# The probabilities of 16 attention units scaled by a plain multiplication instead of one that also sums

## The chip, the cores and the metric

One core of a Trainium2 chip runs the whole program in one launch. The metric is the device time in microseconds, from the median of several runs. Five engines work side by side, each through its own queue in order: TensorE (PE, and PEld for its weight loads), VectorE (DVE), ScalarE (ACT), GpSimd (POOL) and SyncE (SP), which here only issues transfers.

## What is computed

The reference chains three blocks over 4 batches of 576 tokens. The attention block has 8 heads of 64 columns and a mask in blocks of 64 tokens; its output feeds a gated two-layer block, and that a second one with a token mix.

```python
scores = scale * np.matmul(q, k.transpose(0, 1, 3, 2))
scores = np.where(mask, scores, -1000000000.0)
scores = scores - np.max(scores, axis=-1, keepdims=True)
attn = np.exp(scores)
attn = attn / (np.sum(attn, axis=-1, keepdims=True) + 1e-09)
attn_out = np.matmul(attn, v)
# first block (x: attention output, heads side by side; xk, xr: mixes of x and x shifted by a token)
k = np.maximum(xk @ w_k, 0.0)
x = sigmoid(xr @ w_r) * (k * k @ w_v)
# second block
h = gelu(x @ w_in); u, v = split(h)
out = x + (u * (w_sg @ layernorm(v) + b_sg)) @ w_out
```

## The kernel before

**Units.** Attention is cut into 64 units: a batch, a head, and the low (tokens 0 to 319) or high half of its queries. They run in the order low halves of batches 0 and 1 (units 0 to 15), high halves of batches 0 and 1 (16 to 31), then the same for batches 2 and 3. For the first 16 units (`n < DIRECT`, with `DIRECT = 16`) queries and keys are multiplied as plain float32; later ones are split into a rounded part and a remainder, which costs POOL, ACT and DVE more work (`split_qk`, `split_v`).

**One unit.** `emit_S` gives PE the score products in three chunks of 64, 128 and 128 queries. DVE takes the row maximum (L348), ACT scales it (L350) and takes the exponential with its row sum (L355), and `norm` follows on DVE: the row sums get their 1e-9 (L360), the reciprocal is taken (L361), and each chunk of the probabilities P is multiplied in place by its row's reciprocal (L365). That last instruction is `tensor_scalar` with a second operation and `accum_out=junk`: it also writes a row sum, into `junk`, which nothing reads. Then `emit_T` transposes P on PE (L387), ACT copies the result from PSUM to SBUF (L393, recorded at the helper L167), and `emit_PV` multiplies with the values. A P buffer serves every second unit (`P_89` and `P_90` in the listings of the order).

**The first block beside it.** While the first units run, 20 tiles of weights (8 of `w_k`, 4 of `w_r`, 8 of `w_v`) are loaded by SP and split into a float32r pair by `w_split`: ACT takes the absolute value (L228), DVE does two plain one-source instructions (L229, L230) and two with two sources (L232, L234) on 128x512, ACT rounds (L237), and POOL subtracts (L178, `w<-u,w`). The first block's products are then `M<-xh,w` and `M<-xl,w` (with `w_k` and `w_r`) and `M<-kh,w` and `M<-kl,w` (with `w_v`, 96 for each half batch). `xh`/`xl` and `kh`/`kl` are further float32r pairs; POOL and DVE share their remainders (L178), and L501 on DVE mixes the tokens.

**What sets the order.** The program is written in an order that a small planner makes (class `Order`: due times of the work of the other engines against PE's estimated time), and the tile framework's scheduler, with `schedule_with_timeline_sim=True`, then orders every engine's queue by a timeline of its own estimates. When the cost of one kind of instruction changes, rows change places on every engine, far from the edit too. SP's queue is in order as well: a load whose buffer is not yet free holds all loads behind it.

The lines quoted most:

```python
nc.vector.tensor_scalar(out=P[0:m, o:o + e], in0=P[0:m, o:o + e],
                        scalar1=rr[0:m, c:c + 1], scalar2=None, op0=ALU.mult, op1=ALU.add,
                        accum_out=junk[0:m, c:c + 1])                       # L365
nc.vector.tensor_scalar(out=v, in0=v, scalar1=F64_MIN, scalar2=F64_MAX,
                        op0=ALU.max, op1=ALU.min)                           # L229
```

Of the kernel before, what the change touches and what calls it, by code (L numbers as in the profile page):

```python
# [13 lines left out]
ALU = mybir.AluOpType  # L14
# [28 lines left out]
class Order:  # L43
# [12 lines left out]
    def pe(self, ns):  # L56
        self.run(self.t)
        self.t += ns

    def at(self, dt, fn, *keys):  # L60

        heapq.heappush(self.heap, (self.t + dt, self.n, fn))
        for k in keys:
            self.due[k] = max(self.due.get(k, 0.0), self.t + dt)
        self.n += 1
# [38 lines left out]
DIRECT = 16  # L104
# [14 lines left out]
def fused_kernel(ctx: ExitStack, tc: tile.TileContext, first, qkv_lo, qkv_hi, mu,  # L119
                 w_k, w_v, w_r, w_in, g_ln, w_sgT, b_sg, w_out, outT):  # L120
    nc = tc.nc
# [19 lines left out]
    def ptile(tag, cols, bufs):  # L141

        r = ring.setdefault(tag, [])
        if len(r) >= bufs:
            order.need(("ps", tag, len(r) - bufs))
        key = ("ps", tag, len(r))
        r.append(key)
        return ps([128, cols], F32, tag, bufs), key
# [13 lines left out]
    def mm(out, lhsT, rhs, start=False, stop=False):  # L162
        nc.tensor.matmul(out=out, lhsT=lhsT, rhs=rhs, start=start, stop=stop)  # L163
# [141 lines left out]
    def score_ns(n):  # L305
        f, cs = (2, CHUNKS[units[n][2]]) if n >= DIRECT else (4, CHUNKS[LO])
        return sum(f * cost(e - a) for c in cs for a, e in PIECES[c]) + cost(64) * (f == 2) * sum(c > 0 for c in cs)
# [6 lines left out]
    def emit_S(n):  # L314
        b, h, kind = units[n]
        order.need(("sp", n))
        Q, K, KL = splits.pop(n)
        chunks = CHUNKS[kind]
        if n < H and n % 2 and kind == LO:
            (sa, ka), (sb, kb) = ptile("M", 512, 2), ptile("M", 512, 2)  # L320
        else:
            (sa, ka), (sb, kb) = ptile("SA", 512, 1), ptile("SB", 1024, 1)
        stc = {0: sa[:, 0:64], 1: sa[:, 64:256], 2: sb[:, 0:320], 3: sa[:, 0:448]}
        if kind == HI:
            stc[4] = sb[:, 224:800]
        skc = [ka, ka, kb, ka, kb]
        P = probs[n] = pbuf[n % 2]
        pe(score_ns(n))
        mx, sm = smax[n % 4], ssum[n % 4]
        t0, t1 = TOKENS[kind]  # L330
        nb = atile([128, 5], F32, "nb", 4)
        rr = atile([128, 5], F32, "rr", 4)
        for c in chunks:
            q0, m, e, st = CH0[c] - TOKENS[kind][0], CHN[c], CHE[c], stc[c]
            for k0, k1 in PIECES[c]:
                o = st[0:m, k0:k1]
                if n < DIRECT:
                    mm(o, Q[:, q0:q0 + m], K[:, k0:k1], start=True, stop=True)
                    continue
                mm(o, Q[:, q0:q0 + m], K[:, k0:k1], start=True)  # L340
                if c > 0 and k1 == e:
                    mm(st[:, e - 64:e], mask_l, mask_r)
                mm(o, Q[:, q0:q0 + m], KL[:, k0:k1], stop=True)

        def red(cs):
            for c in cs:
                m, e, st = CHN[c], CHE[c], stc[c]
                nc.vector.tensor_reduce(out=mx[0:m, c:c + 1], in_=st[0:m, 0:e], axis=AX.X, op=ALU.max)  # L348
            s = slice(cs[0], cs[-1] + 1)
            nc.scalar.activation(out=nb[:, s], in_=mx[:, s], func=AF.Copy, scale=-0.125)  # L350

        def exp(cs):
            for c in cs:
                m, e, st, po = CHN[c], CHE[c], stc[c], POFF[c]
                nc.scalar.activation(out=P[0:m, po:po + e], in_=st[0:m, 0:e], func=AF.Exp,  # L355
                                     scale=0.125, bias=nb[0:m, c:c + 1], accum_out=sm[0:m, c, 0:1])

        def norm():
            cs = slice(chunks[0], chunks[-1] + 1)
            nc.vector.tensor_reduce(out=rr[:, cs], in_=sm[:, cs], axis=AX.X, op=ALU.add)  # L360
            nc.vector.reciprocal(out=rr[:, cs], in_=rr[:, cs])  # L361
            for c in chunks:
                m, e, o = CHN[c], CHE[c], POFF[c]

                nc.vector.tensor_scalar(out=P[0:m, o:o + e], in0=P[0:m, o:o + e],  # L365
                                        scalar1=rr[0:m, c:c + 1], scalar2=None, op0=ALU.mult, op1=ALU.add,
                                        accum_out=junk[0:m, c:c + 1])

        parts = [[0, 1, 2]] if kind == LO else [[3], [4]]
        t = 0  # L370
        for cs in parts:
            w = sum(CHE[c] for c in cs)
            sk = [skc[c] for c in cs]
            at(t, lambda cs=cs: red(cs), *sk)
            t += 1.1 * w
            at(t + 100, lambda cs=cs: exp(cs), *sk, ("P", n))
        at(t + 1.2 * w + 500, norm, ("P", n))

    def emit_T(n, u):
# [608 lines left out]
```

## Time and profile before

| | |
|---|---|
| median of 3 runs | 714.28 us (713.51 to 714.79) |
| span of the profiled execution | 713.7 us |
| PE busy | 681.8 us (96% of the span) |
| DVE busy | 533.7 us (75%) |
| ACT busy | 435.7 us (61%) |
| POOL busy | 328.0 us (46%) |

The profile records one execution. Its own time outside the span is not given; the median of the runs lies 0.6 us above the span, and that difference is used as what lies around it. The page gives busy time by engine, a strip of 40 slices, the chain of work that ended last, and the costliest groups of instructions; the trace behind it answers questions on single lines, stretches and instructions. In its rows "idle before" in square brackets is the time for which the engine stood still just before the instruction, and the arrow names what ended it.

### The profile page before, as it was taken

What the parts mean: (1) busy time and instruction counts of PE and PEld (TensorE: products, weight loads), DVE (VectorE), ACT (ScalarE), POOL (GpSimd) and SP (SyncE); (2) the same over time, 40 slices, a digit from 0 to 9 for tenths busy, and PEclk for the clock granted to TensorE, in tenths of its full rate; (3) what the DMA queues carried; (4) which work ended last, traced back from release to release, by engine and by line L of the source; (5) the groups of instructions that cost most, each with busy time, mean ns of one, the idle gap of its engine ahead of it and who ended that gap; (6) DMA issues with size and microseconds to landing.
All of it is one profiled execution on the core that took longest, in us unless ns stands there. A gap on an engine that the chain in (4) does not pass through costs nothing.

```text
span 713.7 us, 13603 instructions
## 1 busy us (share of the span) xinstructions
PE 681.8 (96%) x4824; PEld 646.5 (91%) x4824; DVE 533.7 (75%) x1306; ACT 435.7 (61%) x1247; POOL 328.0 (46%) x381
## 2 busy tenths in 40 slices
PE   7888889999999999999999999989999999999998
PEld 4567778999899999999999999979889998999998
DVE  5989998888897786787898977499798446446223
ACT  4978876976897797897897697364443122022020
POOL 1437748854694485675585483061224013013020
PEclk9999999999999999999999999999999999999999
DMA  8681125122322323223223310342910120120202
GB/s 250 252 270 38 35 69 181 51 85 92 109 63 77 98 67 87 75 91 117 84 67 105 96 68 1 101 170 92 327 62 3 56 75 1 59 75 1 67 1 67
DMA packets 30723, 65.78 MB, mean 92 GB/s; under 512 B 5280, under 2 KB 16544, under 8 KB 30656
## 3 DMA queue, kind: packets, MB, share of 16 engines
q1 hardware_dynamic: 30512, 64.91, 28.1%
q8 instruction: 38, 0.62, 0.4%
q14 instruction: 29, 0.24, 0.1%
q10 hardware_dynamic: 144, 0.00, 0.0%
HBM read 55.47 MB, written 9.44 MB: 91 GB/s over the span
## 4 chain that ended last, share of the span: by engine, by line
PE 65%; DVE 15%; DMA 8%; ACT 6%; issue 3%; POOL 2%; SPq 0%; POOLq 0%; DVEq 0%; ACTq 0%
PE M L163 36%; PE O L163 13%; PE V L163 5%; PE T L387 5%; PE SA L163 3%; PE SB L163 3%; DMA w<-w_v_dram 2%; DVE u L232 2%; DMA w<-w_k_dram 2%; DVE u L234 2%; DVE t L501 2%; DVE P L365 2%; ACT P L355 2%; DMA xtr<-x2d 1%; DMA w<-w_out_dram 1%
## 5 line engine op out<-in xcount | busy, mean ns | idle before, releaser
L163 PE MATMUL M<-xh,w 128*128 128x288 f32 x704 | 160.0, 302 | 3.3 <-ACT xh L167 2.2
L163 PEld LDWEIGHTS M<-xh,w 128*128 128x128 f32 x704 | 117.8, 189 | 5.0 <-ACT xh L167 2.4
L163 PE MATMUL M<-xl,w 128*128 128x288 f32 x352 | 104.5, 298 | 0.8 <-DVE xl L178 0.3
L163 PE MATMUL M<-kh,w 128*128 128x288 f32 x432 | 100.1, 302 | 1.1 <-POOL w L178 1.0
L387 PE MATMUL T<-ident,P 128*128 128x128 f32 x480 | 81.7, 281 | 5.7 <-DVE P L365 5.6
L178 DVE TENSOR_TENSOR PL<-T,PH 128x256 fp32r<-128x256 f32 (+3 forms) x128 | 69.0, 543 | 18.0 <-ACT PH L167 17.1
L365 DVE TENSOR_SCALAR_CACHE_REDUCE P<-P,rr 64x64 f32<-64x64 f32 (+3 forms) x160 | 79.3, 537 | 1.3
L167 ACT ACTIVATE PH<-T 128x384 fp32r<-128x384 f32 (+4 forms) x144 | 67.9, 478 | 19.3 <-PE T L387 18.4
L866 POOL TENSOR_TENSOR gt<-gt,U 128x288 f32<-128x288 f32 x32 | 29.3, 919 | 100.9 <-DVE gt L862 100.8
L178 POOL TENSOR_TENSOR KL<-qkv,K 128x576 fp32r<-128x576 f32 (+1 forms) x48 | 61.5, 1282 | 28.2 <-ACT K L167 23.0
L163 PEld LDWEIGHTS M<-kh,w 128*128 128x128 f32 x432 | 72.5, 188 | 1.9 <-POOL w L178 1.8
L387 PEld LDWEIGHTS T<-ident,P 128*128 128x128 f32 x480 | 59.6, 145 | 10.9 <-issue 7.3
L163 PEld LDWEIGHTS M<-xl,w 128*128 128x128 f32 x352 | 66.3, 188 | 1.7 <-DVE xl L178 0.9
L178 POOL TENSOR_TENSOR V<-qkv,V 128x320 fp32r<-128x320 f32 (+1 forms) x48 | 38.7, 805 | 60.8 <-ACT V L167 43.8
L178 POOL TENSOR_TENSOR kl<-R,kh 128x288 fp32r<-128x288 f32 x64 | 58.5, 920 | 14.7 <-ACT kh L167 13.2
L163 PE MATMUL M<-kl,w 128*128 128x288 f32 x216 | 64.3, 298 | 0.0
L178 POOL TENSOR_TENSOR w<-u,w 128x512 fp32r<-128x512 f32 x24 | 35.6, 1484 | 57.3 <-ACT w L237 57.2
L178 POOL TENSOR_TENSOR xl<-t,xh 128x288 fp32r<-128x288 f32 x48 | 41.1, 857 | 41.3 <-ACT xh L167 38.3
L163 PE MATMUL O<-PH,V 128*128 128x256 f32 (+2 forms) x208 | 57.5, 285 | 1.1 <-DVE xT L439 1.0
L163 PE MATMUL O<-PL,V 128*128 128x256 f32 (+2 forms) x208 | 55.1, 281 | 0.8 <-DVE PL L178 0.8
L163 PE MATMUL M<-XHL,w 128*128 128x288 f32 x384 | 53.4, 295 | 1.0 <-ACT U L834 1.0
L834 ACT ACTIVATE U<-M 128x288 f32<-128x288 f32 x32 | 13.0, 410 | 66.2 <-PE M L163 66.2
(188 smaller groups left out, 1960.0 us busy)
## 6 DMA issues: line engine op xcount, KB each, us to landing
qkv<-qkv_hi_dram SPq DMA_DIRECT2D x32, 576.0 KB, 3.9
qkv<-qkv_lo_dram SPq DMA_DIRECT2D x16, 416.0 KB, 3.2
x2d<-x SPq DMA_DIRECT2D x32, 144.0 KB, 2.0
X<-x2d SPq DMA_DIRECT2D x4, 1152.0 KB
outT_dram<-o SPq DMA_DIRECT2D x32, 144.0 KB, 1.8
w<-w_k_dram SPq DMA_DIRECT2D x8, 512.0 KB
w<-w_v_dram SPq DMA_DIRECT2D x8, 512.0 KB, 8.0
w<-w_in_dram SPq DMA_DIRECT2D x8, 512.0 KB, 4.2
```

The lines of the kernel that those rows point to most:

```text
L163: nc.tensor.matmul(out=out, lhsT=lhsT, rhs=rhs, start=start, stop=stop)
L167: nc.scalar.activation(out=out, in_=in_, func=AF.Copy)
L178: eng.tensor_tensor(out=out, in0=a, in1=b, op=ALU.subtract)
L232: nc.vector.scalar_tensor_tensor(out=u, in0=high, scalar=-0x40000000, in1=u, op0=ALU.bitwise_and, op1=ALU.bitwise_or)
L234: nc.vector.scalar_tensor_tensor(out=u, in0=low, scalar=29, in1=u, op0=ALU.logical_shift_right, op1=ALU.bitwise_or)
L355: nc.scalar.activation(out=P[0:m, po:po + e], in_=st[0:m, 0:e], func=AF.Exp, scale=0.125, bias=nb[0:m, c:c + 1], accum_out=sm[0:m, c, 0:1])
L365: nc.vector.tensor_scalar(out=P[0:m, o:o + e], in0=P[0:m, o:o + e], scalar1=rr[0:m, c:c + 1], scalar2=None, op0=ALU.mult, op1=ALU.add, acc ...
L387: nc.tensor.transpose(t[:, o:o + 128], P[:, POFF[c] + CH0[j]:POFF[c] + CH0[j] + 128], ident)
L501: nc.vector.scalar_tensor_tensor(out=t1, in0=x[:, s0 + 1:s0 + 1 + HF], scalar=mu_t[:, i, c:c + 1], in1=t1, op0=ALU.mult, op1=ALU.add)
L834: nc.scalar.activation(out=U[b][:, m, fs], in_=p, func=AF.Gelu_apprx_tanh)
L866: nc.gpsimd.tensor_tensor(out=gt, in0=gt, in1=U[b][:, m, fs], op=ALU.mult)
```

## The change

For the first 16 units the multiplication by the reciprocal is now the same instruction without the second operation and without the accumulator. Three instructions in each of 16 units take the new form, 48 of the 160 that L365 issued; the other 112 keep the old one. The code behind the edit stands four lines lower, so that L365 of before is L366 (plain) and L369 (with the sum) of after, and L387 is L391.

```diff
             for c in chunks:
                 m, e, o = CHN[c], CHE[c], POFF[c]
 
+                if n < DIRECT:
+                    nc.vector.tensor_scalar(out=P[0:m, o:o + e], in0=P[0:m, o:o + e],
+                                            scalar1=rr[0:m, c:c + 1], scalar2=None, op0=ALU.mult)
+                    continue
                 nc.vector.tensor_scalar(out=P[0:m, o:o + e], in0=P[0:m, o:o + e],
                                         scalar1=rr[0:m, c:c + 1], scalar2=None, op0=ALU.mult, op1=ALU.add,
                                         accum_out=junk[0:m, c:c + 1])
```

The scheduler moves other rows with it. On DVE, at the end of the low units, `rr` and `P_90` are those of unit 15, `u<-u` and `u<-w,u` the splits of the last weight tiles. Before:

```order
L348 TENSOR_REDUCE stats<-SB 128x1
L234 SCALAR_TENSOR_TENSOR u<-w,u 128x512
L229 TENSOR_SCALAR u<-u 128x512
L230 TENSOR_SCALAR u<-u 128x512
L501 SCALAR_TENSOR_TENSOR t_1409<-xT,mu_t,t_1409 128x288
L232 SCALAR_TENSOR_TENSOR u<-w,u 128x512
L169 CAST K<-qkv 128x576
L234 SCALAR_TENSOR_TENSOR u<-w,u 128x512
L360 TENSOR_REDUCE rr<-sums 128x3
L361 RECIPROCAL rr<-rr 128x3
L365 TENSOR_SCALAR P_90,junk<-P_90,rr 64x64
```

Now:

```order
L234 SCALAR_TENSOR_TENSOR u<-w,u 128x512
L360 TENSOR_REDUCE rr<-sums 128x3
L361 RECIPROCAL rr<-rr 128x3
L366 TENSOR_SCALAR P_90<-P_90,rr 64x64
L366 TENSOR_SCALAR P_90<-P_90,rr 128x192
L366 TENSOR_SCALAR P_90<-P_90,rr 128x320
L169 CAST K<-qkv 128x576
L229 TENSOR_SCALAR u<-u 128x512
L505 SCALAR_TENSOR_TENSOR t_1396<-xT,mu_t,t_1396 128x288
L230 TENSOR_SCALAR u<-u 128x512
```

Unit 15 is scaled behind 18 of the 20 weight tiles now, where it stood behind all 20.

On PE the six transposes of unit 15 (`T<-ident,P_90`) stood among the products with `w_v` before, behind 42 of them:

```order
L163 MATMUL M<-kh,w 128x288
L163 MATMUL M<-kl,w 128x288
L163 MATMUL M<-kh,w 128x288 x2
L387 MATMUL T<-ident,P_90 128x128 x6
L163 MATMUL M<-kh,w 128x288
```

They stand ahead of all of them now, right behind the output products of unit 14:

```order
L163 MATMUL O<-PL_1226,qkv 128x320
L163 MATMUL O<-PL_1232,qkv 128x256
L163 MATMUL O<-PL_1232,qkv 128x128
L391 MATMUL T<-ident,P_90 128x128 x6
L163 MATMUL M<-kh,w 128x288
L163 MATMUL M<-kl,w 128x288
```

All products with `w_v` of the first half batch now wait for unit 15 on PE.

On SP, `qkv_143` is the load for unit 7, `qkv_371` for unit 8, `qkv_426` for unit 9, and `w_463` and `w_488` are two tiles of `w_v`; rows with - stood there before, rows with + stand there now:

```order
 L271 DMA qkv_143<-qkv_lo_dram 128x256
+L219 DMA w_463<-w_v_dram 128x1024
+L219 DMA w_488<-w_v_dram 128x1024
 L270 DMA qkv_371<-first_dram 66x640
 L271 DMA qkv_371<-qkv_lo_dram 128x256
-L219 DMA w_463<-w_v_dram 128x1024
-L219 DMA w_488<-w_v_dram 128x1024
 L270 DMA qkv_426<-first_dram 66x640
```

The two weight tiles are issued ahead of unit 8's load now. From the second block on, PE's order is the same in both kernels.

## Rows read from the trace of the kernel before

**Rows 1.** The page: span, and busy time of each engine.
```profile
span 713.7 us, 13603 instructions
...
PE 681.8 (96%) x4824; PEld 646.5 (91%) x4824; DVE 533.7 (75%) x1306; ACT 435.7 (61%) x1247; POOL 328.0 (46%) x381
```
**Rows 2.** Stretches: length, busy PE, PEld, DVE, ACT, POOL, clock, DMA, GB/s.
```profile
20.00:55.00 35.00, 28.26 (x139) 20.34 (x138) 31.93 (x105) 29.51 (x92) 12.91 (x11) 0.95 0.68 242
55.00:113.00 58.00, 50.12 (x308) 42.76 (x306) 54.30 (x125) 45.45 (x134) 39.86 (x34) 0.97 0.18 52
113.00:714.00 601.00, 587.82 (x4336) 572.68 (x4336) 436.13 (x1033) 351.54 (x992) 271.72 (x314) 1.00 0.25 81
```
**Rows 3.** Order of time on DVE, unit 10: start, duration, instruction.
```profile
67.33 0.27 DVE L365 TENSOR_SCALAR_CACHE_REDUCE P<-P,rr 64x64 f32<-64x64 f32 x1
...
67.86 0.53 DVE L365 TENSOR_SCALAR_CACHE_REDUCE P<-P,rr 128x320 f32<-128x320 f32 x1
...
68.33 0.47 DVE L348 TENSOR_REDUCE stats<-SA 64x1 f32<-64x64 f32 x2
```
**Rows 4.** Single lines with the plain form: ns minimum/median/maximum, first and last start.
```profile
L229 DVE TENSOR_SCALAR u<-u x32: 398/421/1110, 12.9 to 527.2; 128x512 f32<-128x512 f32 x32
...
L640 DVE TENSOR_SCALAR um_t<-mu_t x1: 173/173/173, 4.0 to 4.0; 128x8 f32<-128x8 f32 x1
...
L800 DVE TENSOR_SCALAR vt<-vt,ag,rs x18: 529/544/1484, 504.1 to 661.1; 128x512 f32<-128x512 f32 x18
```
**Rows 5.** Groups by shape up to 55 us, then 55 to 107: busy us, mean ns.
```profile
L365 DVE TENSOR_SCALAR_CACHE_REDUCE P<-P,rr 128x320 f32<-128x320 f32 x10 | 5.3, 533 | 0.0
L229 DVE TENSOR_SCALAR u<-u 128x512 f32<-128x512 f32 x10 | 4.5, 452 | 1.0 <-ACT u L228 0.9
L230 DVE TENSOR_SCALAR u<-u 128x512 int32<-128x512 int32 x9 | 4.4, 484 | 0.1
...
L229 DVE TENSOR_SCALAR u<-u 128x512 f32<-128x512 f32 x10 | 6.6, 659 | 0.0
L230 DVE TENSOR_SCALAR u<-u 128x512 int32<-128x512 int32 x11 | 5.8, 530 | 0.2
L365 DVE TENSOR_SCALAR_CACHE_REDUCE P<-P,rr 128x320 f32<-128x320 f32 x6 | 3.2, 533 | 0.0
```
**Rows 6.** Order of time on DVE and POOL at 70 us.
```profile
69.56 1.11 DVE L229 TENSOR_SCALAR u<-u 128x512 f32<-128x512 f32 x1
...
68.73 1.66 POOL L178 TENSOR_TENSOR w<-u,w 128x512 fp32r<-128x512 f32 x1
```
**Rows 7.** Order of time around 40 to 53 us on SP, PE and DVE.
```profile
37.75 0.31 SPq L270 DMA_DIRECT2D qkv<-first_dram  x1
...
38.49 0.90 SPq L219 DMA_DIRECT2D w<-w_v_dram  x2
40.68 0.31 SPq L270 DMA_DIRECT2D qkv<-first_dram  x1
...
47.46 0.82 PE L163 MATMUL SA<-qkv 66*64 66x64 f32 x4 [1.35 <-DMA qkv<-first_dram]
...
53.03 0.16 DVE L360 TENSOR_REDUCE rr<-sums 128x3 f32<-128x6 f32 x1 [1.46 <-ACT P L355]
```
**Rows 8.** Order of time at the end of the low units: DVE, PE, POOL, and the chain.
```profile
98.98 0.69 DVE L234 SCALAR_TENSOR_TENSOR u<-w,u 128x512 int32<-128x512 int32 x1
...
108.19 0.92 PE L387 MATMUL T<-ident,P 128*128 128x128 f32 x6 [2.01 <-DVE P L365]
...
112.21 0.73 POOL L178 TENSOR_TENSOR Q<-qkv,Q 64x256 fp32r<-64x256 f32 x1
113.02 1.44 POOL L178 TENSOR_TENSOR KL<-qkv,K 128x576 fp32r<-128x576 f32 x1
114.40 1.10 POOL L178 TENSOR_TENSOR V<-qkv,V 128x320 fp32r<-128x320 f32 x1
...
113.50 3.53 PE M L163 x26
```

## The prediction, made before the changed kernel ran

> **What bounds the kernel now.** I read the page first, then the table of stretches, then the order of time in the first 113 us, since all changed instructions lie there. The page says PE: 681.8 of 713.7 us busy [rows 1]. The stretches say where PE is not the bound. From 113 us to the end it is idle for 601.00 - 587.82 = 13.2 us, 2%; from 20 to 113 us it is idle for (35.00 - 28.26) + (58.00 - 50.12) = 14.6 us, 16% [rows 2]. In that first stretch DVE is busy for 31.93 of 35 and 54.30 of 58 us: there DVE sets the pace, with the splits of 20 weight tiles and the normalisation of the first 16 units. POOL, which takes part in those splits, goes from 12.91 of 35 to 39.86 of 58 us. So the change can win no more than those 14.6 us, and only through DVE's queue; everything behind 113 us is a row of PE work that starts earlier or later. The point to watch is the last of the 16 units: its transposes stand at 108.19 us and PE was idle for 2.01 us before them, waiting for L365 [rows 8].
>
> **The change part by part.**
>
> *1. The multiplications themselves.* In unit 10 the three old instructions hold DVE from 67.33 to 68.33, 1.00 us; the longest of them lasts 0.53 us, and the next instruction starts 0.06 us before it is over [rows 3]. No plain multiplication by a column stands in the trace of this stage. The nearest rows are L229, plain with two constants, at best 398 ns for 512 columns, and L800, plain with two columns of scalars, at best 529 ns [rows 4]. Ours has one column of scalars, so 464 ns would be halfway. L640 shows 173 ns for 8 columns, which makes the slope (398 - 173)/504 = 0.45 ns a column [rows 4]. By L229 the three chunks of 64, 192 and 320 columns cost 0.20 + 0.26 + 0.31 us, less 0.06 us of overlap each: 0.59, a saving of 0.41 us a unit. By L800 each costs 0.13 us more: 0.98, a saving of 0.02. Halfway is 0.22; I take 0.3, nearer to L229, since the small L640 makes the slope too flat. 16 x 0.3 = **-4.8 us** (bounds -0.3 and -6.6). It lies on DVE, which is the pace of this stage.
>
> *2. Waiting for POOL.* The old form takes 533 ns for 320 columns both before and after 55 us; L229 goes from its 398 ns to a mean of 452 in the early part and 659 in the late one, L230 to 484 and 530 [rows 5]. One row shows how: L229 at 69.56 lasts 1.11 us and ends at 70.67, after POOL's instruction that runs from 68.73 to 70.39 [rows 6]. A plain DVE instruction waits for POOL's, and the summing form does not. With 398 ns as the undisturbed time of both, the early waits are 54 and 86 ns, mean 0.07 us, the late ones 261 and 132, mean 0.20 us. Ten units lie in the early part and six in the late one: 10 x 3 x 0.07 + 6 x 3 x 0.20 = 2.1 + 3.6 = **+5.7 us**. Bounds: nothing if the short instructions find POOL between its own; 48 x 0.20 = 9.6 us if POOL's work crowds as in the late part all along.
> The Trainium skill has the same rule in "SBUF — State Buffer", section "Who interferes with whom": plain `tensor_scalar`, but not the form that also writes its accumulator, can use the second port, which DVE shares with GpSimd, and whoever comes second blocks until the first is done. By that rule the waits of part 2 are real, and it speaks against this change where POOL is dense; the trace agrees, 533 ns in both stretches for the one form and 452 against 659 for the other. Did the rule not hold here, part 2 would be nothing and the sum -6.2, 708.1 us.
>
> *3. The load of unit 9.* In SP's queue unit 8's load is issued at 37.75, two weight tiles at 38.49, and unit 9's load at 40.68; PE starts unit 9's scores at 47.46, 1.35 us idle for that load, and DVE stands 1.46 us for its exponentials at 53.03 [rows 7]. Now the two tiles go ahead of unit 8's load, whose buffer they need not wait for, so they are under way earlier and out of unit 9's road. What they are moved past is unit 8's own load, which now comes behind them; DVE has weight tiles to split meanwhile. If DVE's wait goes, -1.46; if unit 8 turns late instead, 0. I take **-1.2 us**.
>
> *4. The order at the end of the low units.* Before, PE did 42 products with `w_v` and then unit 15's transposes at 108.19. Products come at 3.53/26 = 0.136 us [rows 8], so 42 are 5.7 us, and with those behind the transposes now, PE is level with before if the transposes start at 108.2 - 5.7 = 102.5. DVE comes to the new place of unit 15, behind 18 tiles, at 98.98 + 0.69 = 99.7 in the old pace [rows 8], and to the end of its scaling 1.0 us later, 100.7: 1.8 us to the good. Against it, POOL's subtraction for the last weight tile now stands behind the three remainders of unit 17, 0.73 + 1.44 + 1.10 = 3.3 us [rows 8], and PE needs it at the end of these products; about half of that is covered by the scores of units 16 and 17. Sum -1.8 + 1.6 = **-0.2 us** (bounds -1.8 and +1.5).
>
> *5. The order behind 113 us.* Rows change places up to the end of attention, at equal work. PE is idle for 13.2 us there [rows 2], in many waits; a new order draws other ones. I take 0, with a fifth of it, 2.5 us, to either side.
>
> Sum: -4.8 + 5.7 - 1.2 - 0.2 + 0 = -0.5 us on a span of 713.7. The span of the profiled execution lies 0.6 us below the median of the runs (714.28), so the forecast is 713.7 + 0.6 - 0.5 = **713.8 us**. A measurement of this kernel tells about 0.2%, 1.4 us, from no change; so this is "no difference that can be told".
>
> **The rivals.**
>
> *A. POOL hardly disturbs the short instructions.* The three follow the reciprocal closely and each is shorter than L229, so only the first of a unit would wait: a third of part 2, 1.9 us. Then -4.8 + 1.9 - 1.2 - 0.2 = -4.3: **710.0 us**. For it: in the early part, with ten of the units, POOL is busy for 12.91 of 35 us. Against it: the late L229 [rows 5].
>
> *B. The shared port becomes the bound.* Between 55 and 113 us POOL is busy for 39.86 of 58 us [rows 2], and the old form left it alone for 1.00 us in each unit. If POOL's backlog is such that each plain instruction waits as in the late part from the start, part 2 is +9.6 and the sum -4.8 + 9.6 - 1.2 - 0.2 = +3.4: **717.7 us, slower**. It decides from about 0.16 us a wait over all 48 (7.6 us), where parts 1 to 4 come to +1.4. It would show at unit 15, whose transposes now hold all products with `w_v`, starting behind 102.5 us.
>
> *C. The new order behind 113 us alone decides*, by 2 us or more to either side: 711.8 or 715.8.
>
> *D. The plain form is no cheaper than the summing one* (saving 0.02 us a unit, by L800) and then waits little, being no faster use of the port: only parts 3 and 4 remain with -0.3 of part 1: 712.6 us, just faster.
>
> **How the numbers follow.** Forecast 0.30; A 0.22; C faster 0.11; D 0.04; B 0.22; C slower 0.11. So faster by over 0.2%: 0.37; within 0.2%: 0.30; slower: 0.33. No case is far ahead, so the range must take in A and B with the order's part around them: 709.0 to 718.5. The forecast's own range is 712.4 to 715.2.
>
> **What would show it.** Part 1: the new line's mean for 64, 192 and 320 columns, undisturbed, near 0.23, 0.30 and 0.36 us, and the three together under 0.8 us. Part 2: its late mean well above its minimum, with POOL rows ending where it ends; if the late units show the minimum throughout, A is right. Part 3: no idle time on PE for `qkv` at 45 to 48 us. Part 4: unit 15's transposes before 102.5 us, and PE without gaps behind them. Part 5: PE's idle time behind 113 us near 13 us. The forecast is wrong if the stage before the `w_v` products ends more than 1.4 us away from where these sums put it, or if PE's idle time behind it moves by more than that.

## The result and the profile after

The changed kernel takes 723.36 us (median of 4 runs, 723.0 to 725.85) against 714.53 us (4 runs): a ratio of 1.0129, 95% interval 1.0108 to 1.015. It is **slower by 1.3%**, 8.8 us, and lies above the range of the prediction.

The page of the profiled execution after, span and busy time (beside [rows 1]):

```profile
span 721.3 us, 13568 instructions
...
PE 685.2 (95%) x4824; PEld 650.1 (90%) x4824; DVE 541.3 (75%) x1258; ACT 435.7 (60%) x1247; POOL 328.4 (46%) x381
```

DVE was to be relieved and is busy for 7.6 us longer. The stretches after, columns as in [rows 2]:

```profile
20.00:55.00 35.00, 26.20 (x131) 19.23 (x129) 34.09 (x82) 28.53 (x85) 14.37 (x12) 0.95 0.71 253
55.00:113.00 58.00, 50.46 (x296) 43.70 (x297) 54.96 (x108) 43.70 (x133) 34.78 (x31) 0.91 0.19 59
113.00:721.00 608.00, 593.07 (x4356) 576.58 (x4354) 442.51 (x1038) 354.42 (x1000) 276.22 (x318) 1.00 0.25 80
```

In the first stretch DVE is busy for 34.09 of 35 us where it was 31.93, and PE did 131 instructions where it did 139. The new line by shape, in the first 55 us and then up to 125 us (busy us, mean ns, idle before):

```profile
L366 DVE TENSOR_SCALAR P<-P,rr 64x64 f32<-64x64 f32 x9 | 4.5, 504 | 0.0
L366 DVE TENSOR_SCALAR P<-P,rr 128x320 f32<-128x320 f32 x8 | 3.0, 372 | 0.0
L366 DVE TENSOR_SCALAR P<-P,rr 128x192 f32<-128x192 f32 x8 | 2.4, 305 | 0.0
...
L366 DVE TENSOR_SCALAR P<-P,rr 128x192 f32<-128x192 f32 x8 | 5.8, 724 | 0.0
L366 DVE TENSOR_SCALAR P<-P,rr 64x64 f32<-64x64 f32 x8 | 5.3, 666 | 0.0
L366 DVE TENSOR_SCALAR P<-P,rr 128x320 f32<-128x320 f32 x8 | 4.2, 524 | 0.0
```

The old form took 533 ns for 320 columns in both parts [rows 5]. The plain form takes 372 ns where nothing disturbs it; behind 55 us it takes as long as the old form there, and for 64 columns 666 ns, where the old one took 0.27 us [rows 3]. The order of time shows what disturbs it: an undisturbed unit on DVE, then unit 12 on DVE and POOL (start, duration; x3 is the three multiplications of a unit).

```profile
10.39 0.77 DVE L366 TENSOR_SCALAR P<-P,rr 64x64 f32<-64x64 f32 x3
11.09 0.47 DVE L348 TENSOR_REDUCE stats<-SA 64x1 f32<-64x64 f32 x2
...
83.16 3.03 DVE L366 TENSOR_SCALAR P<-P,rr 64x64 f32<-64x64 f32 x3
```

And POOL at that time:

```profile
82.65 1.74 POOL L178 TENSOR_TENSOR w<-u,w 128x512 fp32r<-128x512 f32 x1
84.36 0.82 POOL L178 TENSOR_TENSOR xl<-t,xh 128x288 fp32r<-128x288 f32 x1
85.13 0.88 POOL L178 TENSOR_TENSOR kl<-R,kh 128x288 fp32r<-128x288 f32 x1
```

Three POOL instructions end at 84.39, 85.18 and 86.01, and the three multiplications that start at 83.16 end at 86.19: each waited for one POOL instruction, and between two of them POOL took its turn. Undisturbed the three take 0.77 us, and DVE's next instruction starts after 0.70 us.
The Trainium skill says in "SBUF — State Buffer", section "Who interferes with whom", that the shared ports go to one engine for a whole instruction and the other blocks fully; these rows agree, and add that three short instructions in a row can lose three times.

Seven of the 16 units were disturbed: 1.77, 1.18, 1.71, 1.77, 2.91, 3.03 and 2.37 us. With nine at 0.77 that is 21.6, less 16 x 0.07 of overlap 20.5 us, where the old form held DVE for 16 x 1.00 [rows 3]. So the multiplications cost DVE 4.5 us more, not 4.8 less. PE waits for them:

```profile
L366 DVE TENSOR_SCALAR P<-P,rr x48: 238/370/1421, 10.4 to 103.9; 64x64 f32<-64x64 f32 x16, 128x192 f32<-128x192 f32 x16, 128x320 f32<-128x320 f32 x16
...
  PE T L391: 9.2, 10
```

9.2 us in 10 waits, where it waited 5.6 us in 6 before; the longest are 2.25 us at 56.06 and 2.21 us at 94.17. But 4.5 us of DVE are not yet 8.8 us, and three causes were possible: the form, the order that the scheduler made of it, and TensorE's clock, whose mean was 0.988 here and 0.995 in the profiled execution of before.

### The profile page after: what moved, and what is told of

Read it like the earlier page. It is cut to its first block, busy times and chain, and to the rows that moved or that the text cites. A ratio compares the mean times of both kernels' runs of the same rounds, so it can differ in the third digit from the quotient of the medians.

```text
span 721.3 us, 13568 instructions
## 1 busy us (share of the span) xinstructions
PE 685.2 (95%) x4824; PEld 650.1 (90%) x4824; DVE 541.3 (75%) x1258; ACT 435.7 (60%) x1247; POOL 328.4 (46%) x381
## 4 chain that ended last, share of the span: by engine, by line
PE 71%; DVE 15%; DMA 6%; ACT 4%; issue 2%; POOL 1%; SPq 1%; ACTq 0%; DVEq 0%; POOLq 0%
PE M L163 38%; PE O L163 14%; PE T L391 5%; PE V L163 5%; PE SA L163 4%; PE SB L163 4%; DVE u L232 2%; DVE u L234 2%; DVE P L366 2%; DVE u L229 1%; DVE u L230 1%; DMA xtr<-x2d 1%; DMA w<-w_k_dram 1%; DMA w<-w_out_dram 1%; DVE stats L348 1%
## 5 line engine op out<-in xcount | busy, mean ns | idle before, releaser
L163 PE MATMUL M<-xh,w 128*128 128x288 f32 x704 | 161.7, 304 | 7.6 <-ACT R L556 3.7
L163 PE MATMUL M<-kh,w 128*128 128x288 f32 x432 | 98.4, 302 | 0.8 <-ACT w L237 0.8
L391 PE MATMUL T<-ident,P 128*128 128x128 f32 x480 | 81.0, 282 | 9.2 <-DVE P L366 9.2
L391 PEld LDWEIGHTS T<-ident,P 128*128 128x128 f32 x480 | 59.8, 145 | 15.0 <-issue 8.1
L178 POOL TENSOR_TENSOR kl<-R,kh 128x288 fp32r<-128x288 f32 x64 | 56.4, 890 | 18.8 <-ACT kh L167 17.3
L369 DVE TENSOR_SCALAR_CACHE_REDUCE P<-P,rr 128x448 f32<-128x448 f32 (+3 forms) x112 | 62.3, 596 | 1.2
L505 DVE SCALAR_TENSOR_TENSOR t<-xT,mu_t,t 128x288 f32<-128x288 f32 x64 | 50.4, 787 | 4.3 <-ACT t L504 4.0
```

The lines of the kernel that those rows point to most:

```text
L178: eng.tensor_tensor(out=out, in0=a, in1=b, op=ALU.subtract)
L391: nc.tensor.transpose(t[:, o:o + 128], P[:, POFF[c] + CH0[j]:POFF[c] + CH0[j] + 128], ident)
L505: nc.vector.scalar_tensor_tensor(out=t1, in0=x[:, s0 + 1:s0 + 1 + HF], scalar=mu_t[:, i, c:c + 1], in1=t1, op0=ALU.mult, op1=ALU.add)
```

## Experiments

All were timed in five rounds (6 to 12 runs each) against the kernel before on the same chip; before had medians of 715.2 to 715.9 us there. Differences in us below are the ratio less 1, times 715. **How form and order were parted:** the program is scheduled with one form, and only then the finished instructions are exchanged for the other, so that every queue keeps its order row by row.

### 1. Form alone, order alone

```diff
# order of before, plain form (scaled: what L365 returned, with unit n and chunk c)
+    plain = {x.ins.name for n, c, x in scaled if n < DIRECT}
...
+                if x.name in plain:
+                    b.instructions[k] = dataclasses.replace(x, outs=x.outs[:1], op1=ALU.bypass)
# order of after, summing form (scheduled with the plain one)
+                if x.name in chunk:
+                    b.instructions[k] = dataclasses.replace(x, outs=[x.outs[0], junk[chunk[x.name]]], op1=ALU.add)
```

> Order of before, form of after: the program is scheduled with the summing form, and only then the 48 multiplications of the first 16 units lose the second operation and the accumulator, so that every queue keeps the order of the kernel before row by row. Theory PORT (the plain form waits for whole GpSimd instructions, the reciprocal's three multiplications turn late, TensorE waits): the three multiplications still last up to 3 us in the units where GpSimd subtracts weights, and the time is 719 to 724 us. Theory ORDER (the scheduler's new order is what costs): 709 to 715 us, since DVE only gets shorter work. Theory CLOCK (a rider on either): wherever TensorE waits 1 us or more several times between 60 and 130 us, its granted clock there falls to 0.88 to 0.95, and the mean over the span is 0.988 where it does, 0.995 where it does not.

> Order of after, form of before: the program is scheduled with the plain form, and only then the 48 multiplications get the second operation and the accumulator back. PORT: 713 to 716 us, like the kernel before, with multiplications of 0.53 us for 320 columns throughout and a mean granted clock of 0.995. ORDER: 721 to 724 us, like the changed kernel, clock 0.988.

Form alone: 720.63 us, ratio 1.007 (1.005 to 1.009). Order alone: 720.37 us, 1.007 (1.0047 to 1.0093). **Neither theory has it alone:** each costs 5.0 us, and together (10.0) about what both cost in the changed kernel (1.0129, 9.2 us). With the form alone six units are disturbed (order of time on DVE; the first row is one of the ten undisturbed):

```profile
10.34 0.77 DVE L365 TENSOR_SCALAR P<-P,rr 64x64 f32<-64x64 f32 x3
...
18.88 1.78 DVE L365 TENSOR_SCALAR P<-P,rr 64x64 f32<-64x64 f32 x3
24.16 2.40 DVE L365 TENSOR_SCALAR P<-P,rr 64x64 f32<-64x64 f32 x3
33.47 2.40 DVE L365 TENSOR_SCALAR P<-P,rr 64x64 f32<-64x64 f32 x3
...
48.02 2.23 DVE L365 TENSOR_SCALAR P<-P,rr 64x64 f32<-64x64 f32 x3
...
70.32 2.94 DVE L365 TENSOR_SCALAR P<-P,rr 64x64 f32<-64x64 f32 x3
...
112.05 2.12 DVE L365 TENSOR_SCALAR P<-P,rr 64x64 f32<-64x64 f32 x3
```

These are units 2, 3, 4, 7, 10 and 15. All 16 hold DVE for 20.4 us, 4.4 more than the old form, close to the 5.0 us.

### 2. Which units cost, and is it lateness?

The same exchange as for the form alone, in ten units, in the other six, and in nine of the ten; and a kernel with no plain multiplication that is late for another reason:

```diff
+    plain = {x.ins.name for n, c, x in scaled if n in (0, 1, 5, 6, 8, 9, 11, 12, 13, 14)}
+    plain = {x.ins.name for n, c, x in scaled if n in (2, 3, 4, 7, 10, 15)}
+    plain = {x.ins.name for n, c, x in scaled if n in (0, 1, 6, 8, 9, 11, 12, 13, 14)}
# summing form, L360 repeated into unread columns ahead of itself: unit and times
+    times = {2: 5, 3: 9, 4: 9, 7: 8, 10: 12, 15: 7}
```

> Order of before; the plain form only in the ten units 0, 1, 5, 6, 8, 9, 11 to 14, whose three multiplications took 0.76 to 0.85 us, undisturbed, in the run with the order of before and the plain form in all 16. Theory PORT (only the multiplications that meet a GpSimd instruction cost): VectorE's queue is 10 times 0.24 us shorter, 712 to 715.5 us, against 720.6 with all 16 plain. Theory FORM (the plain form costs wherever it stands): ten sixteenths of +5, 717.5 to 719.5 us.

> Order of before; the plain form only in the six units 2, 3, 4, 7, 10 and 15, whose three multiplications took 1.78, 2.40, 2.40, 2.23, 2.94 and 2.12 us in the run with the plain form in all 16 (about 1.0 each in the summing form). PORT: all of the loss is here, 719.5 to 722.5 us. FORM: six sixteenths of +5, 716 to 718 us.

> Order of before; the plain form only in units 0, 1, 6, 8, 9, 11, 12, 13 and 14: the ten of the earlier run without unit 5, whose three multiplications then met GpSimd and took 2.41 us. If each quiet unit gives VectorE 0.3 us and VectorE's queue sets the pace, 9 times 0.3 us off: 711.5 to 714 us, below the kernel before by 0.2 to 0.5 per cent. If other units meet GpSimd instead, or the gain ends in waits for TensorE and the loads: 714.5 to 716 us.

> Order of before, summing form throughout, no plain multiplication: ahead of the reciprocal of units 2, 3, 4, 7, 10 and 15 VectorE repeats the small sum L360 5, 9, 9, 8, 12 and 7 times (0.16 us each) into unread columns, which makes these units late by about as much as the waits of the plain form did, 8 us in all. Theory LATE (what costs is that the scaled probabilities come late, by whatever cause): 719 to 722.5 us, like the plain form in these six units, with two or three more stretches of TensorE at half its clock than the kernel before. If it is the port itself that hurts in another way (GpSimd held up by VectorE, say): 714.5 to 717 us.

Ten quiet units: 714.55 us, ratio 0.9995 (0.9974 to 1.0017). Six disturbed ones: 722.01 us, 1.0104 (1.0078 to 1.013). So PORT holds: the loss sits where POOL is met, and the quiet units cost nothing. Among the ten, one met POOL after all (2.41 us at 35.51); it was unit 6, not unit 5 as the expectation of the nine says, so the nine kept it (2.39 us) and left out a quiet one: 715.14 us, 0.9992 (0.9976 to 1.0009). Neither is a gain that the measurement can tell. The repeated sums: 719.46 us, 1.006 (1.0033 to 1.0088). Unit 10's rows, on DVE and then on PE:

```profile
69.60 0.88 DVE L360 TENSOR_REDUCE junk<-sums 128x3 f32<-128x6 f32 x12
70.40 0.14 DVE L360 TENSOR_REDUCE rr<-sums 128x3 f32<-128x6 f32 x1
```

```profile
71.55 0.52 PE L387 MATMUL T<-ident,P 128*128 128x128 f32 x3 [2.09 <-DVE P L365]
```

Twelve of them take 0.80 us, 0.067 each and not the 0.16 of the expectation, so all 50 are 3.3 us on DVE, for 4.3 us of time. **Lateness as such costs about its own length.** Put side by side, the change of DVE's time in these 16 units and that of the kernel: quiet ten -1.4 (with the one disturbed) and -0.4; nine -1.1 and -0.6; sums +3.3 and +4.3; all 16 +4.4 and +5.0; disturbed six +7.4 and +7.4 (their 13.85 us less 6 x 0.07 and 6 x 1.00).

### 3. Is it the clock?

```diff
# plain form, order of before; the identity is transposed ahead of the first transposes: unit and times
+    fill = {3: 12, 4: 9, 7: 9, 8: 8, 10: 16, 15: 22}
```

> Order of before, plain form in all 16 units; ahead of the first transposes of units 3, 4, 7, 8, 10 and 15, where TensorE stood 1.3 to 3.2 us for the scaling, it first transposes the identity 12, 9, 9, 8, 16 and 22 times (about 0.13 us each at full clock), into the buffer that the real transposes overwrite. It cannot start the real ones earlier. Theory CLOCK (a good part of the loss is that TensorE runs at half its clock after it stood): 715.5 to 718.5 us, with the stretches at half clock behind these places gone. Theory IDLE (the wait itself is the whole loss): 720 to 721.5 us, as without them.

720.10 us, ratio 1.0079 (1.0054 to 1.0105): no better than without them. The filling did its work, as unit 10 shows; PE in this kernel, in order of time:

```profile
71.70 1.91 PE L387 MATMUL T<-ident 128*128 128x128 f32 x16
74.33 0.52 PE L387 MATMUL T<-ident,P 128*128 128x128 f32 x3 [0.71 <-DVE P L365]
```

The stretch behind the same wait (columns as in [rows 2]) in the kernel without the filling, experiment 1:

```profile
72.00:77.00 5.00, 4.97 (x22) 4.98 (x23) 4.90 (x8) 2.34 (x8) 3.45 (x4) 0.50 0.00 0
```

And with it:

```profile
74.00:79.00 5.00, 4.67 (x34) 4.52 (x35) 4.93 (x9) 3.03 (x13) 3.44 (x5) 1.00 0.00 0
```

Here the filling ends 0.71 us before the probabilities come, so it holds nothing up, and the stretch behind it runs at a granted clock of 1.00 where it was 0.50, the lower of the two levels. Over the six executions the mean clock was 0.991 to 0.998, against 0.985 to 0.988 without the filling, and the time is the same. **CLOCK falls as it was put (715.5 to 718.5 us), and the time is that of IDLE:** with this order and full work PE has slack up to 113 us, and what it wins at full clock it spends waiting for DVE. A share of one or two microseconds is not excluded by the two intervals. At unit 3 of the profiled execution the scaling was over at 28.06 us, and the filling, which began at 28.38, held the real transposes up until 30.01; the granted clock was 0.50 from 23 to 29 us all the same. Nor was the filling tried in the new order. The kernel before, too, had 0.986 to 0.993 in the eleven executions beside experiment 1; the 0.995 of its profiled execution was above all of them, and the two profiles' clocks had suggested a larger difference than the runs show.

### 4. With GpSimd's weight work taken away

GpSimd only writes zeros for the remainders of the 20 weight tiles, which leaves them out of the result; all else is as in experiments 1 and 2, in both orders.

```diff
-    (GpSimd) w_lo = u - w_hi        # L242 in these kernels, 20 tiles
+    (GpSimd) w_lo = 0
```

> Order of before, plain form, and GpSimd's subtraction for the 20 weight tiles of the first block (1.3 to 1.7 us each in the kernel before) is replaced by one that only writes zeros, so the remainders of these weights are left out of the result. To be read against the same edit with the summing form. PORT: most of the multiplications find GpSimd idle, so this kernel is 0 to 5 us faster than its partner, where the plain form with the full subtraction is slower than the kernel before. ORDER: the plain form gains the same against its partner as in the run with the full subtraction.

> Order of before, summing form, GpSimd only writes zeros for the remainders of the 20 weight tiles (left out of the result): the partner of the run above. PORT and ORDER alike: 711 to 715 us; shorter work on GpSimd frees L229 and L230, plain as well, from waits of 0.05 to 0.26 us on the mean, 20 tiles times up to 0.4 us on DVE, of which TensorE sees a part.

> Order of before; GpSimd only writes zeros for the remainders of the 20 weight tiles (left out of the result); plain form in units 0 to 14, summing form in unit 15. With the plain form in unit 15 too this was 710.0 us, with the summing form in all 707.1. In the first of these unit 15 alone met long GpSimd work (three multiplications in 2.12 us, while the other 15 units took 0.76 to 1.16 us). Theory UNIT 15 (its lateness is the whole difference): 704.5 to 707.5 us. If the plain form costs something in undisturbed units too: 708.5 to 710.5 us.

> Order of the changed kernel, summing form, and GpSimd only writes zeros for the remainders of the 20 weight tiles (left out of the result). The same with the order of before was 707.1 us; with the full subtraction the two orders were 715.6 and 720.4. Theory MEET (the new order costs because under it VectorE's splits and mixes meet GpSimd's subtractions more often: their time up to the last weight tile is 1.7 us longer in the summing form, and the last weight tile is ready 2.2 us later): the difference between the orders shrinks to under 2 us, 705.5 to 709.5 us. Theory QUEUE (the new order costs by what stands in front of what in TensorE's queue, whatever GpSimd does): 711 to 713.5 us.

> The changed kernel itself with GpSimd's subtraction for the 20 weight tiles replaced by a write of zeros (their remainders left out of the result). With the order of before and the plain form this was 710.0 us, with the full subtraction the changed kernel is 723.4. MEET: 707 to 711.5 us. QUEUE: 712.5 to 716.5 us.

| us against the kernel before | order of before | order of after |
|---|---|---|
| full work, summing form | 0 | +5.0 |
| full work, plain form | +5.0 | +9.2 |
| short work, summing form | -8.1 (707.08 us, 0.9862 to 0.9912) | -1.3 (714.14 us, 0.9961 to 1.0003) |
| short work, plain form | -5.7 (709.96 us, 0.9899 to 0.9941) | -3.2 (712.77 us, 0.9937 to 0.9974) |

With full work the form costs 5.0 and 4.2 us; with short work +2.4 and -1.9, on the average nothing. So its cost shrinks by 2.6 us in the one order and 6.1 in the other when GpSimd's weight work goes, which bears out GpSimd as the cause of most of it. Two expectations missed: in the order of before the plain form is 2.9 us slower than its partner, not 0 to 5 us faster, and the summing form with short work is below its 711 to 715 us. **The order costs about as much with short work** (+6.8 and +2.5, mean 4.7): MEET falls and QUEUE is nearer, though the summing kernel lies above its 711 to 713.5 us.

One thing stays open in part: with short work and the order of before the plain form did not gain, though its 16 units took DVE 2.7 us less. Unit 15 was suspected (2.12 us in that run), but with the summing form there it is 709.57 us, 0.991 (0.9885 to 0.9936), the same. The two profiled executions, 5.1 us apart and with the same order on PE, show where the kernels part. At unit 10 the plain form meets POOL and PE waits for 1.47 us, with the summing form 0.92; the clock falls behind the longer wait, and behind unit 10 the plain form is 2.2 us late (last section). What parts them behind that was not followed up.

### 5. Where in the order?

All with the summing form and full work. The order of after is kept up to a unit and another follows; it was got by scheduling with the plain form in the first 14, 10 or 4 units. In the last one the order of after is whole, and the three GpSimd instructions between the last two weight subtractions write zeros (the remainders of Q, K and V of unit 17 are left out).

```diff
+    scheduled with the plain form: n < 14
+    scheduled with the plain form: n < 10
+    scheduled with the plain form: n < 4
-    (GpSimd, unit 17) Q_lo = q - Q, K_lo = k - K, V_lo = v - V
+    (GpSimd, unit 17) Q_lo = 0, K_lo = 0, V_lo = 0
```

> Summing form throughout, in an order that is row by row that of the changed kernel on TensorE up to the first transposes of unit 14 and another one behind: unit 15's transposes stand behind 15 of the products with w_v instead of ahead of all of them, and the scores of the next units come elsewhere. (The program was scheduled with the plain form in units 0 to 13, and the multiplications got the second operation back afterwards.) To be read against the run with the changed kernel's whole order and the summing form, 720.4 us. Theory END (the end of the low units is where that order loses: the last weight tiles come late on GpSimd and the scores stand in TensorE's queue ahead of what is ready): 715 to 717.5 us. Theory EARLY (the order of the first 14 units loses): 719.5 to 721.5 us.

> Summing form throughout; TensorE's order is that of the changed kernel up to the first transposes of unit 9, and another one behind (scheduled with the plain form in units 0 to 9, which got the second operation back afterwards). Whole changed order: 720.4 us; order of before: 715.2. If the loss lies in units 0 to 9: 719 to 721.5 us. If it lies in units 10 to 14: 714.5 to 717.5 us, unless the order behind draws a loss of its own.

> Summing form throughout; TensorE's order is that of the changed kernel up to the transposes of unit 4, and another one behind (scheduled with the plain form in units 0 to 3, which got the second operation back afterwards). If the loss lies in units 0 to 4: 719 to 721.5 us. If it lies in units 5 to 9: 714.5 to 717.5 us here, and 719 to 721.5 in the run that keeps the changed order up to unit 9.

> Order of the changed kernel, summing form, full weight subtractions; only the three GpSimd instructions that stand between the last two of the 20 weight subtractions (the remainders of Q, K and V of unit 17, 1.06, 1.52 and 1.07 us in the run with this order) write zeros instead, so these three remainders are left out of the result. Without this edit the kernel took 720.4 us, the kernel before 715.6. Theory END (the new order loses where the last weight tile and unit 17's scores wait for GpSimd, the 3.3 us that the prediction counted half): 716 to 718.5 us. Theory EARLY (the loss lies in the first 14 units, as the median of the run with another end suggests): 719.5 to 721 us.

Kept to unit 14: 720.12 us, ratio 1.0059 (1.0039 to 1.0078). To unit 9: 720.58 us, 1.0064 (1.0043 to 1.0084). To unit 4: 719.34 us, 1.0049 (1.003 to 1.0067). Short remainders of unit 17: 720.46 us, 1.0073 (1.0048 to 1.0099). Four different ends, one loss of 3.5 to 5.2 us. By these times END falls: what the four share is the order of the first units, and shorter remainders of unit 17 win nothing. PE in the first units, in order of time, in the kernel that keeps the order to unit 14:

```profile
33.95 1.46 PE L163 MATMUL O<-PL,qkv 128*128 128x320 f32 x6 [1.12 <-ACT xT L167]
37.24 1.46 PE L163 MATMUL O<-PH,qkv 128*128 128x320 f32 x6 [0.67 <-ACT PH L167]
39.86 0.92 PE L387 MATMUL T<-ident,P 128*128 128x128 f32 x6 [1.16 <-DVE P L365]
44.58 0.40 PE L163 MATMUL M<-xh,w 128*128 128x288 f32 x1 [1.28 <-ACT P L355]
```

The six output products of a unit stand together here, and PE waits for ACT and DVE at each turn, 4.2 us in four waits. The whole order of after (experiment 1), the kernel kept to unit 9 and the one with short remainders have the same four waits within 0.01 us; the one kept to unit 4 has others (1.27 us at 35.19, 1.04 at 38.34).

The profiles do not show the loss there, though. PE's work up to 113 us and behind it (columns as in [rows 2]) in the kernel before:

```profile
0.00:113.00 113.00, 93.99 (x489) 73.83 (x489) 97.60 (x275) 84.18 (x256) 56.30 (x67) 0.97 0.46 149
113.00:125.00 12.00, 12.00 (x91) 11.94 (x92) 11.26 (x27) 7.95 (x23) 9.22 (x8) 1.00 0.69 226
```

And in the order of after with the summing form (experiment 1):

```profile
0.00:113.00 113.00, 93.52 (x489) 74.32 (x489) 99.53 (x274) 84.89 (x256) 54.59 (x68) 0.97 0.47 157
113.00:125.00 12.00, 11.29 (x63) 10.72 (x62) 9.88 (x25) 6.96 (x19) 6.97 (x8) 0.72 0.40 137
```

Up to 113 us PE has done 489 instructions in both (of unlike length; it was busy for 93.99 and 93.52 us), so what it lost in the first units it has made up by then: before, it waits elsewhere, 2.01 us for unit 15 alone [rows 8]. From 113 to 125 us it does 91 and 63. Kept to unit 14 these numbers are 488 and 80, to unit 9 481 and 53, to unit 4 485 and 55, with short remainders 489 and 69. What PE waits for there in the order of after:

```profile
110.53 0.40 PE L163 MATMUL M<-kh,w 128*128 128x288 f32 x1 [0.82 <-ACT w L237]
112.66 0.44 PE L163 MATMUL SA<-K,Q 128*128 128x448 f32 x1 [1.21 <-POOL KL L178]
114.13 0.61 PE L163 MATMUL SB<-K,Q 128*128 128x288 f32 x1 [0.71 <-ACT P L355]
```

These are the last weight tiles, a split of K and the exponentials, 2.74 us in all, and from 114 to 120 us the granted clock is 0.50, where before it was 1.00. With short remainders the waits are 0.81, 0.82 and 0.94 us, and the clock falls to 0.72. The kernel kept to unit 14 waits for 1.66 and 2.22 us, keeps a clock of 1.00, and its profiled span is 715.2 us, only 1.5 above that of before, with the four waits of the first units as they are; but this was the fastest of its ten runs. So the times of the runs point at the first units, the profiles, of one execution each, at 110 to 125 us, the clock included. **That the order costs 5.0 us is shown; where in it they arise is not:** no run had the order of before in one of these stretches alone.

## Why the prediction was wrong, point by point

**What bounds the kernel: right in the place, wrong in one conclusion.** The time is decided ahead of 120 us through DVE's queue, and lateness there costs its length (experiment 2). But from the 14.6 us I concluded only what the change can win: a reordering can also lose there, which had no term.

**Part 1, the multiplications themselves (-4.8): right.** Undisturbed they take 0.70 us a unit against 1.00, with 305 ns for 192 columns and 372 ns for 320 (forecast 0.30 and 0.36 us); 16 x 0.30 is 4.8 us. The 0.3 was a choice between bounds of 0.02 and 0.41, so some luck is in the exact hit.

**Part 2, waiting for POOL (+5.7): the mechanism right, the size wrong.** Measured +9.4 us: the seven disturbed units' 14.7 us less 7 x 0.77. That is the upper bound, 9.6, and the price of rival B. The step that failed here is the wait per instruction, 0.07 us early and 0.20 us late, taken as a mean from L229 [rows 5]. L229 stands alone; these stand three in a row, and a unit that meets POOL at all loses 0.4 to 2.3 us. Nor are the early units quiet: with the form alone, four of the six disturbed units lie ahead of 55 us, where POOL is busy for only 12.91 of 35 us [rows 2].

**Part 3, the load of unit 9 (-1.2): not found.** The two weight tiles do go ahead, but PE still waits for a first load, 1.35 us, only later. SP, after (beside [rows 7]):

```profile
36.42 0.91 SPq L219 DMA_DIRECT2D w<-w_v_dram  x2
38.97 0.32 SPq L270 DMA_DIRECT2D qkv<-first_dram  x1
```

And PE:

```profile
63.91 0.82 PE L163 MATMUL SA<-qkv 66*64 66x64 f32 x4 [1.35 <-DMA qkv<-first_dram]
```

**Part 4, the end of the low units (-0.2): the gain right for the order alone, the price too low.** The break-even for unit 15's transposes was 102.5 us, and the part had its scaling end at 100.7. In the new order with the summing form the transposes start at 100.39 (experiment 1), as the part said. In the changed kernel they start at 106.16: its scaling starts at 103.51, behind a wait of 1.44 us for ACT and behind the disturbed units 11 to 13. The last weight tile on POOL starts at 117.42, behind the three remainders, as the part said. DVE, after:

```profile
103.10 0.16 DVE L360 TENSOR_REDUCE rr<-sums 128x3 f32<-128x6 f32 x1 [1.44 <-ACT P L355]
103.30 0.18 DVE L361 RECIPROCAL rr<-rr 128x3 f32<-128x3 f32 x1
103.51 0.77 DVE L366 TENSOR_SCALAR P<-P,rr 64x64 f32<-64x64 f32 x3
```

And POOL:

```profile
116.39 1.07 POOL L178 TENSOR_TENSOR V<-qkv,V 128x320 fp32r<-128x320 f32 x1
117.42 1.48 POOL L178 TENSOR_TENSOR w<-u,w 128x512 fp32r<-128x512 f32 x1
```

The part took 1.6 us for that. In the order alone PE waits for 2.74 us at 110.5 to 114.1 and then runs at the lower clock (experiment 5); with the remainders shortened the time stayed, so they alone are not the reason.

**Part 5, the order behind 113 us (0 with 2.5 to either side): within its bound, but it was given all of the order's spread.** PE's idle time behind 113 us is 608.00 - 593.07 = 14.9 us against 13.2 [rows 2], 1.7 more. The order alone costs 5.0 us (experiment 1), where parts 3 to 5 have -1.4. **This is the step that failed most:** of the new order I priced the two places where I saw a row move, took both for gains, and gave a spread only to the part behind 113 us. Where in the order the 5.0 us arise stays open (experiment 5).

**The sum, mended:** -4.8 + 9.4 + 5.0 = +9.6 on 714.3 gives 723.9; measured 723.4. These terms were measured afterwards, in part in other kernels.

**The rivals.** B had the right mechanism and price, and its sign came: unit 15's transposes start behind 102.5 us. It lay 5.7 us too low, since it took -1.4 for parts 3 and 4, where the order costs 5.0. A and D are excluded by the rows of the triples, C by its place: PE's idle time behind 113 us grew by 1.7 us of the 8.8. The clock, which the prediction left out, explains no large part of what the form costs (experiment 3); what it does in the new order was not tried.

## What to carry to other kernels

An instruction that gets faster by taking a resource that another engine holds is priced by whole instructions of that engine wherever the two can meet, and three in a row can meet up to three of them; the mean wait of a lone instruction is too low a price. Here the slower form used nothing shared, and not even the units that POOL left alone gained a time that the measurement can tell, so it should have been left. Where a scheduler orders by its own costs, a change of one instruction's cost is two changes: exchange the form after scheduling and time them apart, and give the whole reordered stretch a spread of its own, here 5 us of 715. And do not read a difference between two profiles' mean clocks as a cause before several executions of each show it.

## What was not expected of the hardware

Three short plain multiplications on DVE (238 to 372 ns) took up to 3.03 us, with single ones up to 1421 ns in the changed kernel, as POOL's instructions took turns with them. TensorE's granted clock fell to its lower level behind some waits and not behind others: with short work and the old order, the kernel with the plain form waited 1.47 us and then ran at half speed (the next products start 0.39 and 0.24 us apart):

```profile
65.73 0.67 PE L387 MATMUL T<-ident,P 128*128 128x128 f32 x3 [1.47 <-DVE P L365]
66.05 0.59 PE L163 MATMUL M<-xh,w 128*128 128x288 f32 x1
66.44 0.44 PE L163 MATMUL M<-xl,w 128*128 128x288 f32 x1
```

Its partner with the summing form waited 0.92 us and kept its speed (0.21 us apart; the next again 0.13):

```profile
65.10 0.52 PE L387 MATMUL T<-ident,P 128*128 128x128 f32 x3 [0.92 <-DVE P L365]
65.38 0.38 PE L163 MATMUL M<-xh,w 128*128 128x288 f32 x1
65.59 0.29 PE L163 MATMUL M<-xl,w 128*128 128x288 f32 x1
```

Yet before, a wait of 2.01 us at 108.19 [rows 8] was followed by no such fall (1.00 from 80 to 125 us).

Where PE has no slack the lower clock costs time of its own. The same two kernels from 65 to 70 us, plain form, then summing form:

```profile
65.00:70.00 5.00, 4.27 (x22) 4.29 (x23) 4.90 (x11) 3.21 (x10) 4.00 (x5) 0.66 0.01 2
65.00:70.00 5.00, 4.90 (x35) 4.72 (x36) 4.90 (x10) 4.61 (x16) 3.27 (x4) 1.00 0.00 2
```

The transposes start 0.63 us apart, the output products behind them 2.17 us (at 71.14 and 68.97). From 70 to 98 us PE is busy for 28.00 of 28 us in both, so nothing of this is regained there. A second pair has the order of after on PE, once as in experiment 1 and once with short remainders. Behind waits of 2.02 and 1.79 us for the same ACT line (L552) the granted clock from 417 to 421 us is 0.57 in the one and 1.00 in the other, and the distance between them grows from 1.26 us (416.14 and 414.88) to 2.79 (421.83 and 419.04). In experiment 3, where PE had slack, a higher clock won nothing. How much of the 8.8 us comes by the clock is not settled: of the 21 executions of the kernel before that ran beside experiment 5's first kernel, the eight at 0.992 and more had a mean span of 712.7 us, the nine at 0.988 and less 714.8, which may be the waits as well as the clock.
